# Segment 0 of a segmented-attention block: whole instead of halves, queries and keys in w2's space, scores in loose bank pairs, a new instruction order

## The chip, the core and the metric

The kernel runs on one core of one Trainium2 chip, in one launch. The metric is the device time of one execution in microseconds (us). A core has five engines with a queue each: TensorE (PE, matmuls into the eight PSUM banks; its weight loads are shown as PEld), VectorE (DVE), ScalarE (ACT), GpSimd (POOL) and SyncE (SP, which here issues DMAs). Each works through its own queue in order, and semaphores order the engines among themselves.

## The reference

One transformer block over 2048 tokens of width 640, with 32 heads of 20 columns and a feed-forward width of 1728. Attention runs in four segments of 512 tokens: causal softmax inside the segment, plus a linear memory `M`, `z` that the earlier segments have filled.

```python
x = A_x
h = x + _A_ref(_layernorm(x), wq, wk, wv, wo, beta)
h2 = h + silu(_layernorm(h) @ w1) @ w2

# inside _A_ref, for each segment s (q, k, v are the segment's)
p = softmax(q @ k.T * scale + mask)
a_dot = p @ v
num, den = phi(q) @ M, phi(q) @ z + 1e-06      # phi(t) = t + 1 if t > 0 else exp(t)
o = g * num / den + (1 - g) * a_dot            # g = sigmoid(beta)
M, z = M + phi(k).T @ v, z + sum(phi(k))
return concat(o) @ wo
```

For segment 0 the memory is empty, so only `a_dot` counts.

## The kernel before

**How the work is written down.** `build` declares tasks (a few instructions on one engine, with what they read and write) in a `Graph`. The order in which tasks are issued, the buffer each one takes and the engine of those that may run on several are written out by hand in the string `ORDER`; `Graph.schedule` reads it row by row. A row such as `qe011/D:0` is: task `qe011`, on VectorE (A ScalarE, D VectorE, G GpSimd, S SyncE), with buffer 0. `Tracker.add` then finds the semaphore waits from the regions that tasks read and write. So the order on each engine's queue is that of `ORDER`, and it never changes while the kernel runs.

**The tasks of one segment** (numbers in names: segment, then block or chunk; groups are numbered 0 to 31, eight to a segment, four heads to a group):

- `n1_st`, `n1_rs`, `n1_ap` (lines 706 to 723): layer norm of a block of 128 tokens on VectorE and GpSimd. It is transposed into `xT` by TensorE (`n1_tp`, `n1_te`, lines 732 and 741) for segment 0, by a DMA (`n1_tr`, line 747) for the others.
- `v`, `ve` (774, 784): values of a block, ten matmuls of 320 columns, and their copy into `Vx`.
- `pr`, `qe` (808, 816): one chunk of queries or keys, five matmuls of 512 columns, and its copy into `QK` on ScalarE or VectorE.
- `ex`, `ph` (823, 830, 833): phi of a chunk, an exponential on ScalarE, then a maximum (830) and a minimum of two tensors (833) on VectorE.
- `vt` (844): twelve DMA copies per segment on SyncE's queue that gather the last 12 heads' rows from `QK` into `QKV`. Groups 5 to 7 of a segment read `QKV`, groups 0 to 4 `QK`.
- `qk`, `e`, `mk` (880, 891, 903): one score visit, four heads side by side on TensorE into four adjoining PSUM banks; two exponentials on ScalarE, a pair of banks each, into a probability buffer; the causal mask on GpSimd.
- `av`, `oe`, `tn`, `nm`, `ad` (926, 939/941, 955 and 959, 972 to 1000): probabilities times values, copy out, turn to tokens (with the memory part, from segment 1 on), division, sum into `otok`.
- `kt`, `mz`, `ma`, `mb` (1040 to 1084): a DMA transpose of phi(k), and the memory's update.
- `ot`, `wo`, `rs`, `n2_*` (1101 to 1117): transpose of `otok`, output projection, residual, second layer norm into `hT`.
- `h1`, `th`, `s`, `h2`, `o`, `out` (1138/1143, 1152, 1158, 1178, 1195, 1200): the feed-forward layer and the store. `h1_0_7_1` is segment 0, chunk 7, second half.

**Segment 0 is split in halves.** Its first 256 queries see only two key blocks. They have visits of their own (`0x` to `7x`, 384 columns a head, buffers `PTE`), and the other 256 queries two visits a group (`ya`, 512 columns, `PTA`; `yb`, 384 columns, `PTB`). So there are 24 visits, 16 products `av` and 16 copies `oe`, and the first layer of segment 0's feed-forward part also comes in halves of 256 tokens (`parts` in `declare_back`). From segment 1 on a group has visit `a` (512 columns), `b` (384 and 128), and every second group a visit `e` (256 for this group and 256 for the next).

**Buffers.** `PTA`, `PTB` and `PTE` have two slots each. `QK` and `xT` have one copy; a chunk of segment 1 is written into `QK` only when segment 0's visits and copies have read it. A visit asks for four adjoining banks:

```python
sca = G.alloc("ps", nr)          # nr = 4
```

**The start.** SyncE issues x blocks 0 and 1, wv, x blocks 2 and 3, beta, wq and wk, one after the other. wq and wk come raw into `sT`'s space and are rearranged (`re_`, lines 677 and 679) on ScalarE or VectorE. `fill` tasks (line 599) are matmuls of 256 columns on a tile of zeros (`zpad`), whose results nobody reads: 41 in all, 21 of them ahead of the first transpose.

Of the kernel before, what the change touches and what calls it, by code (L numbers as in the profile page):

```python
# [358 lines left out]
zpad:0 x0:0 x1:1 w_wv:0 x2:2 x3:3 beta w_q:0 w_k halfc warm:0 iota vpad0 sel n1_st0:0 n1_st1:1 epsc mt3 vpad1 n1_rs0  # L359
n1_rs1 epsg0 n1_ap0:0 fill21:0 n1_tp0:0 n1_te0/A:0 n1_ap1:1 fill6:2 n1_tp1:2 n1_te1/A v00:0 v01:2 n1_st2:2 n1_rs2  # L360
n1_st3:3 n1_rs3 mt1 mt2 mta1 n1_ap2:2 n1_ap3:3 n1_tp2:4 n1_te2/D re_wq1/A:0 fill4:6 n1_tp3:6 n1_te3/A pr010:6
re_wk1/D:0 re_wk0/D re_wk3/D x4/S:4,5,6,7 pr011:4 re_wk2/D re_wq4/D qe011/D:0 ve00/A:0 re_wk4/A qe010/A re_wq2/A
lsc0 pr001:0 ve01/D lsc1 lsc2 re_wq0/A qe001/A:0 qk1x0:4 e1x2:0 pr000:1 qe000/D lsc3 pr021:0 e1x0 mk1x qk0x0:4
pr020:2 ex001:0 qe021/A:0 e0x2:1 e0x0 qe020/A n1_st5:4 n1_st6:5 pr041:0 re_wq3/D av1x:3 qk2x0:4 w_wo/S:0
x8/A:8,9,10,11 vt06:0 vt00 vt03 vt09 qe041/D:0 pr031:1 pr030:0 n1_st4:6 n1_st7:7 w_w1_0/A:0 mk0x e2x2:0 oe1x/D:0
e2x0 ex041:1 qe030/D:0 qk0yb0:4 pr040:2 w_w1_1/S qe031/A qe040/D mk2x e0yb2:0 e0yb0 n1_rs5 av2x:0 av0x:3 tn1x:1
nm1x:0,0 oe0x/A:1 mk0yb n1_rs6 mtb1 qk1yb0:4 vt010 oe2x/D:0 vt08 vt05 vt02 vt07 vt04 e1yb2:1 e1yb0 ex021:2 zf0 v03:2
qk3x0:4 v02:0 e3x0:0 e3x2 n1_ap6:0 n1_ap5:1 ve03/D n1_tr5:0 vt011 vt01 qk4x0:4 ve02/D tn0x:2 e4x2:1 nm0x:1 e4x0 mm5
n1_rs4 fill6:3 qk0ya0:0 mta3 mk3x e0ya0:0 n1_rs7 ph001:0 mk4x e0ya2 n1_tr6 av3x:4 oe3x/D:1 n1_st8:0 ph021:1 n1_ap4:2
n1_st11:1 fill4:5 qk1ya0:4 e1ya0:1 zf1 e1ya2 v11:0 ve11/A:1 av4x:2 qk5x0:4 tn2x:3 e5x2:0 e5x0 nm2x:2 v12:0 n1_tr4  # L370
n1_ap7:3 epsg1 oe4x/D:0 ve12/D kt02:0 n1_tr7 w_w1_2/S w_w2_0/S kt00:1 w_w1_3/S ex011:0 mk1yb mk5x mt0 qk6x0:4 av0y:2
e6x0:1 e6x2 tn4x:3 oe0y/D:0 av5x:0 tn3x:1 oe5x/A:1 qk7x0:4 e7x2:0 e7x0 nm4x:3 v10:2 nm3x:0 qk2ya0:4 ph041:2
n1_st10:2 ve10/D e2ya0:0 e2ya2 n1_rs11 mta2 mk7x n1_st9:3 n1_rs10 v13:0 mk6x tn0y:2 av7x:3 ve13/D nm0y:1 qk2yb0:4
oe7x/A:0 e2yb2:0 e2yb0 tn5x:3 tn7x:0 nm7x:2 av1y:1 av6x:2 qk3ya0:4 oe6x/D:1 nm5x:3 w_w1_4/S tn6x:2 nm6x:0 ot1:0
w_w2_5/S ot0 w_w2_4/S w_w2_1/S oe1y/A:0 e3ya0:1 e3ya2 ph011:1 pr101:1 mtb3 mz02:2 mk2yb av2y:3 qk3yb0:4 e3yb0:1
e3yb2 ma02/D:0 mz00:2 tn1y:0 oe2y/D:1 n1_ap11:1 qe101/D:0 pr100:3 qk4ya0:4 e4ya0:0 e4ya2 mk3yb ex031:2 nm1y:1
qe100/D wo1:0 av3y:3 qk4yb0:4 e4yb2:0 e4yb0 ma00/D:1 tn2y:2 ex101:1 rs1 wo0:0 oe3y/D:0 n2_st1:5 nm2y:2 kt04:0 tn3y:3
n2_rs1 nm3y:3 rs0 qk5ya0:4 pr140:2 n1_rs8 mk4yb pr121:3 e5ya0:1 e5ya2 qe140/A:0 qk5yb0:4 e5yb2:1 e5yb0 ex140:0
pr141:0 av4y:2 n2_ap1:0 n2_st0:4 n2_rs0 n2_ap0:2 kt01:1 n2_tr1:0 qk6ya0:4 qe141/D mk5yb pr120:1 ph031:0 oe4y/D:1
pr111:0 qe121/D:0 e6ya0:0 e6ya2 qk6yb0:4 qe120/D ex121:2 av5y:3 n2_tr0 h1_0_7_0:1 h1_0_0_0:2 e6yb2:0 e6yb0 qk7ya0:4  # L380
# [24 lines left out]
e16e0 ad15 mk16b th0_5_1:0 mk16a qk17b0:0 vt211:0 ot6:0 s0_5_1 ph211:1 wo6:4 th0_11_1:1 s0_11_1 rs6 n2_st6:1 e17b2:1
# [48 lines left out]
def build(nc, es, A_x, A_wq, A_wk, A_wv, A_wo, A_beta, B_x, B_w1, B_w2, out):  # L454
# [303 lines left out]
    def declare_front(s):  # L758
# [4 lines left out]
        for i in range(4):  # L763
            layer_norm("n1_", 4 * s + i, X[4 * s + i], [0], xTa, xT, i, k0 + P["ln1"] + P["ln1s"] * i if s else -30 + i)
# [491 lines left out]
```

## Time and profile before

| what | value |
|---|---|
| runs of the kernel (device time) | 306.14, 306.86, 307.66 us |
| median | 306.86 us |
| span of the profiled execution, first to last instruction | 305.4 us |
| mean granted TensorE clock in that span | 0.994 |
| instructions: PE, DVE, ACT, POOL | 2876, 490, 322, 280 |
| score exponentials on ScalarE | 168: 136 of 1024 elements, 32 of 768 |
| their mean | 1027 and about 807 ns |
| TensorE's granted clock from 10 to 20 us | 0.83 |
| DMA: bytes and mean rate | 24.65 MB, 81 GB/s |

The profiled execution's span is the time between its first and its last instruction; the device time also holds what lies around them. The page gives busy time by engine, and the same in 40 slices of the span; the chain of waits follows the last instruction back through what released each step; rows by line give the number of instructions, their mean duration and what ended the engine's idle time before them. Matmuls overlap, so the duration of one is longer than the distance from its start to the next one's start.

### The profile page before, as it was taken

How to read it: one execution, taken by the hardware profiler on the slowest of the kernel's cores; microseconds unless marked ns; L12 is line 12 of the kernel's file. 1: busy time of each engine (PE TensorE's matmuls, PEld its weight loads, DVE VectorE, ACT ScalarE, POOL GpSimd, SP SyncE). 2: the span in 40 equal slices, each digit the busy share in tenths (PEclk: the TensorE clock that was granted, in tenths of full speed). 3: DMA queues.
4: the chain of work that ended last, by engine and by line, in shares of the span. 5: the costliest groups of instructions: out<-in, count | busy, mean ns of one | idle time of the engine just before them, and what ended most of it. 6: DMA issues, size and time to landing. Idle time of an engine off the chain costs nothing.

```text
span 305.4 us, 7240 instructions
## 1 busy us (share of the span) xinstructions
PE 291.0 (95%) x2876; PEld 166.5 (55%) x2900; DVE 218.7 (72%) x490; ACT 227.0 (74%) x322; POOL 143.5 (47%) x280
## 2 busy tenths in 40 slices
PE   8699898999999999999999999999999999999996
PEld 6434454555655445656654444556564466764574
DVE  5567999796788895877989878449776476934523
ACT  4488998999998979989889899978878951004410
POOL 4227754433687856536747419334973730300000
PEclk9899999999999999999999999999999999999999
DMA  6658468642264040055552400034250004242001
GB/s 197 211 195 239 75 166 223 127 97 42 90 105 80 17 62 2 1 91 76 114 146 63 67 17 19 2 64 69 39 108 2 0 2 88 64 88 86 0 24 64
DMA packets 48578, 24.65 MB, mean 81 GB/s; under 512 B 38881, under 2 KB 47457, under 8 KB 48545
## 3 DMA queue, kind: packets, MB, share of 16 engines
q1 hardware_dynamic: 47872, 23.09, 33.1%
q10 hardware_dynamic: 672, 1.10, 1.1%
q8 instruction: 23, 0.38, 0.5%
q14 instruction: 11, 0.08, 0.1%
HBM read 10.41 MB, written 2.62 MB: 43 GB/s over the span
## 4 chain that ended last, share of the span: by engine, by line
PE 72%; ACT 12%; DVE 7%; DMA 4%; issue 2%; POOL 1%; SPq 1%; DVEq 0%; ACTq 0%
PE ps_all L1178 18%; PE ps_all L1143 16%; PE ps_all L808 12%; PE ps_all L1109 7%; PE ps_all L880 6%; PE ps_all L926 5%; ACT PTA L891 4%; ACT PTB L891 3%; DMA sT<-in_A_wq_dram 3%; PE ps_all L774 2%; PE ps_all L955 2%; ACT PTE L891 2%; DMA oT<-otok 1%; PE ps_all L959 1%; PE ps_all L1048 1%
## 5 line engine op out<-in xcount | busy, mean ns | idle before, releaser
L891 ACT ACTIVATE PTA<-ps_all 128x1024 bf16<-128x1024 f32 x64 | 62.1, 1027 | 7.1 <-PE ps_all L880 6.5
L1178 PE MATMUL ps_all<-w_sb,sT 128*128 128x320 bf16 x448 | 65.2, 299 | 0.0
L891 ACT ACTIVATE PTB<-ps_all 128x1024 bf16<-128x1024 f32 (+1 forms) x64 | 58.9, 970 | 5.9 <-PE ps_all L880 5.6
L1143 PE MATMUL ps_all<-hT,w_sb 128*128 128x512 bf16 (+1 forms) x315 | 60.1, 335 | 0.9 <-issue 0.5
L1152 ACT ACTIVATE th<-ps_all 128x512 f32<-128x512 f32 (+2 forms) x70 | 34.0, 507 | 34.5 <-PE ps_all L1143 26.8
L1158 DVE SCALAR_TENSOR_TENSOR sT<-th,ps_all 128x512 bf16<-128x512 f32 (+2 forms) x70 | 38.0, 561 | 26.1 <-ACT th L1152 25.0
L903 POOL TENSOR_SCALAR_AFFINE_SELECT PTB<-PTB 128x512 bf16<-128x512 bf16 x64 | 41.2, 644 | 32.7 <-ACT PTB L891 30.4
L1178 PEld LDWEIGHTS ps_all<-w_sb,sT 128*128 128x128 bf16 x448 | 42.3, 98 | 19.3 <-issue 2.1
L1143 PEld LDWEIGHTS ps_all<-hT,w_sb 128*128 128x128 bf16 x325 | 30.3, 98 | 23.9 <-issue 1.3
L891 ACT ACTIVATE PTE<-ps_all 128x1024 bf16<-128x1024 f32 (+1 forms) x40 | 35.4, 943 | 2.2 <-PE ps_all L880 2.1
L903 POOL TENSOR_SCALAR_AFFINE_SELECT PTE<-PTE 128x512 bf16<-128x512 bf16 x40 | 25.9, 647 | 21.0 <-ACT PTE L891 19.5
L706 DVE BATCH_NORM_STATS2 stt<-x_tok 128x6 f32<-128x320 bf16 x64 | 27.9, 477 | 1.5 <-DMA x_tok<-in_A_x_dram 1.3
L808 PE MATMUL ps_all<-xT,wqr 128*128 128x512 bf16 x92 | 24.3, 391 | 3.2 <-ACT xT L741 2.4
L1109 PE MATMUL ps_all<-wo_sb,oT 128*128 128x320 bf16 x160 | 24.1, 299 | 1.0 <-DMA oT<-otok 0.7
L774 PE MATMUL ps_all<-wv_sb,xT 128*128 128x320 bf16 x160 | 24.3, 300 | 0.7 <-DMA xT<-xn_rot 0.5
L808 PE MATMUL ps_all<-xT,wkr 128*128 128x512 bf16 x94 | 24.0, 386 | 0.5 <-issue 0.3
L1000 POOL TENSOR_TENSOR otok<-on 128x320 bf16<-128x320 bf16 x24 | 19.0, 792 | 11.3 <-DVE on L992 11.3
L903 POOL TENSOR_SCALAR_AFFINE_SELECT PTA<-PTA 128x512 bf16<-128x512 bf16 x24 | 15.5, 645 | 16.6 <-ACT PTA L891 16.4
L1195 DVE SCALAR_TENSOR_TENSOR x_tok<-ps_all,x_tok 128x640 bf16<-128x640 f32 (+1 forms) x17 | 13.2, 780 | 14.1 <-PE ps_all L1178 14.0
L880 PE MATMUL ps_all<-QK 20*128 20x256 bf16 (+3 forms) x360 | 20.5, 286 | 1.7 <-ACT PTB L891 0.7
L992 DVE TENSOR_TENSOR on<-ps_all,rd 128x640 bf16<-128x640 f32 x24 | 19.8, 825 | 0.8
L817 DVE CAST QK<-ps_all 128x512 bf16<-128x512 f32 x24 | 16.3, 687 | 5.5 <-PE ps_all L808 5.1
(79 smaller groups left out, 403.5 us busy)
## 6 DMA issues: line engine op xcount, KB each, us to landing
out_dram<-x_tok SPq DMA_DIRECT2D x15, 160.0 KB, 1.9
w_sb<-in_B_w_dram SPq DMA_DIRECT2D x4, 432.0 KB, 5.8
w_sb<-in_B_w_dram SPq DMA_DIRECT2D x3, 480.0 KB, 4.3
x_tok<-in_A_x_dram SPq DMA_DIRECT2D x2, 640.0 KB, 4.7
QKV<-QK SPq DMA_DIRECT2D x16, 72.0 KB
wv_sb<-in_A_wv_dram SPq DMA_DIRECT2D x1, 800.0 KB, 4.9
sT<-in_A_wq_dram SPq DMA_DIRECT2D x1, 800.0 KB, 8.2
sT<-in_A_wk_dram SPq DMA_DIRECT2D x1, 800.0 KB, 9.9
```

What stands on the lines that cost most here:

```text
L706: T.add(DV, lambda e, hh=hh: e.bn_stats(out=stt[:, s, 6 * hh:6 * hh + 6], in_=xb[:, 320 * hh:320 * hh + 320]), reads=R((xa, xsub)), writes ...
L774: fns.append(lambda e, c=c, hh=hh: e.matmul(bank(ps, hh)[:, 0:320], lhsT=xT[:, c, 128 * i:128 * i + 128], rhs=wv_sb[:, c, 320 * hh:320 * h ...
L808: fns = [lambda e, kc=kc: e.matmul(bank(ps)[:, lo:hi], lhsT=wt[:, kc, c, :], rhs=xT[:, kc, lo:hi], start=(kc == 0), stop=(kc == NC - 1)) f ...
L880: fns.append(lambda e, j=j, o=o, r=r, q0=q0, q1=q1, qa=qa, ka=ka: e.matmul(ps_all[:, o:o + q1 - q0], lhsT=ka[32 * r:32 * r + DH, 128 * j:1 ...
L891: T.add(AC, lambda e: e.activation(out=pt[:, pta.slot, q0:q0 + 2, 0:width], in_=sc3[:, b0:b0 + 2, 0:width], func=ACT.Exp, scale=SCALE), re ...
L903: fns.append(lambda e, v=v: e.affine_select(out=v, in_=v, pattern=[[0, 4], [1, 128]], compare_op=ALU.is_ge, fill=0.0, base=0, channel_mult ...
L992: T.add(DV, lambda e: e.tensor_tensor(out=on[:, ona.slot, :, :].rearrange("p b (x e) -> p b x e", e=DH), in0=v[:, :, :, 0:DH], in1=r2.unsq ...
L1109: fns.append(lambda e, c=c, hh=hh: e.matmul(bank(ps, hh)[:, 0:320], lhsT=oT[:, c, 128 * i:128 * i + 128], rhs=wo_sb[:, c, 320 * hh:320 * h ...
L1143: fns = [lambda e, c=c: e.matmul(bank(ps)[:, lo:hi], lhsT=w1_sb[:, c, 128 * f:128 * f + 128], rhs=hT[:, c, lo:hi], start=(c == 0), stop=(c ...
L1152: T.add(AC, lambda e: e.activation(out=th[:, tha.slot, lo:hi], in_=bank(ps)[:, lo:hi], func=ACT.Tanh, scale=0.5), reads=R((ps, [0])), writ ...
L1158: T.add(DV, lambda e: e.scalar_tensor_tensor(out=sT[:, f, lo:hi], in0=th[:, tha.slot, lo:hi], scalar=1.0, in1=bank(ps)[:, lo:hi], op0=ALU. ...
L1178: fns.append(lambda e, f=f, t0=t0, fr=fr, hh=hh: e.matmul(bank(ps, hh)[:, 0:320], lhsT=sT[:, f, t0:t0 + 128], rhs=w2_sb[:, fr, 320 * hh:32 ...
```

## The change

**Segment 0 whole.** The halves are gone: segment 0 has the visits `a`, `b` and `e` of the other segments, 20 instead of 24, eight products and eight copies, and its feed-forward layer has 512 tokens to a matmul.

**Where its operands lie.** The transposed input of segment 0 goes into `hT` instead of `xT`, and its queries and keys into the first eight chunks of `w2_sb`, so that segment 1's can be written while segment 0's are read. The loads of w2 (`load_w2`) are declared behind segment 0's groups, and the first three of them wait for all readers of these queries and keys.

**Scores.** A visit takes two pairs of adjoining banks, wherever they lie, and each exponential reads one pair. The three kinds of probability buffer become one pool of seven.

**Other engines.** The maximum of phi is a task of its own (`pa`), on VectorE or GpSimd; the minimum is `pb`. The rearrangements of wq and wk may run on GpSimd, and four do.

**A new `ORDER`.** All rows are new. The four x blocks are loaded first, then wv, wk, wq, then x blocks 4 to 7, then beta. Of 49 fills 40 stand ahead of the first transpose, and the zero tile is written after the identity matrix. The feed-forward part of segment 0 begins behind the first visit of segment 1's sixth group; before, it began during segment 0's visits.

```diff
-zpad:0 x0:0 x1:1 w_wv:0 x2:2 x3:3 beta w_q:0 w_k halfc warm:0 iota vpad0 sel n1_st0:0 n1_st1:1 epsc mt3 vpad1 n1_rs0
-n1_rs1 epsg0 n1_ap0:0 fill21:0 n1_tp0:0 n1_te0/A:0 n1_ap1:1 fill6:2 n1_tp1:2 n1_te1/A v00:0 v01:2 n1_st2:2 n1_rs2
...
+mt2:0 iota sel zpad x2:2 n1_st2:7 mt0 x0:0 n1_st0:0 warm:0 mta0 epsc halfc n1_rs2 n1_ap2:3 x1:1 x3:3 fill40:0 n1_tp2:3
+n1_st1:1 n1_rs0 n1_ap0:2 w_wv:0 n1_te2/A:0 fill9:0 n1_tp0:4 w_k:0 n1_st3:2 n1_te0/A v02:0 vpad0 ve02/A:0 n1_rs1
+n1_ap1:0 n1_rs3 n1_ap3:3 n1_tp1:6 w_q v00:2 n1_te1/A mt1 re_wk0/D:0 n1_tp3:6 vpad1 v01:0 x4/S:4,5,6,7 n1_te3/D pr001:4
+re_wq0/D:0 pr000:5 re_wq4/D mt3 mta3 re_wk3/G re_wq2/D re_wk2/D beta re_wq3/G ve00/A v03:2 re_wq1/A qe001/A:0 re_wk4/G
+mta1 ve01/A n1_st4:0 ve03/D qe000/A qk0a0:0,4 n1_st5:4 ex001:1 re_wk1/G pr011:7 qe011/D:0 e0a2:5 qk0b0:2,4 mtb1 mtb0
...
+        "QZ0": 1, "QZ1": 1, "QZ2": 1, "QZ3": 1, "QZ4": 1,
-        "PTA": 2, "PTB": 2, "PTE": 2, "oTs": 2, "on": 2, "rd": 4, "otok": 1, "oT": 1,
+        "PT": 7, "oTs": 2, "on": 2, "rd": 4, "otok": 1, "oT": 1,
...
+    QK0 = w2_sb[:, 0:8, :].rearrange("p f e -> p (f e)").rearrange("p (c w t) -> p c w t", c=5, w=2)
...
-            G.task(f"re_{k}{c}", {DV: 0.36 if c < 3 else 0.42, AC: 0.72}, emit, rr, ww, prio + c)
+            G.task(f"re_{k}{c}", {DV: 0.36 if c < 3 else 0.42, AC: 0.72, PO: 0.8 if c < 3 else 0.9}, emit, rr, ww, prio + c)
...
-        xTa = G.alloc("xT")
+        xTa = G.alloc("xT" if s else "hT")
+        xt = xT if s else hT
+        qkt = QK if s else QK0
...
-        qk = [G.alloc(f"QK{c}") for c in range(5)]
+        qk = [G.alloc(f"QK{c}" if s else f"QZ{c}") for c in range(5)]
...
-                    G.task(f"ph{s}{c}{w}", {DV: 0.92}, e_phi, [(qk[c], wall), (exa, [0])], [(pa, ["a"])], prp)
+                    G.task(f"pa{s}{c}{w}", {DV: 0.37, PO: 0.65}, e_pa, [(qk[c], wall)], [(pa, ["a"])], prp)
+                    G.task(f"pb{s}{c}{w}", {DV: 0.38}, e_pb, [(exa, [0]), (pa, ["a"])], [(pa, ["a"])], prp)
...
-                sca = G.alloc("ps", nr)
+                sca = [G.alloc("ps", 2) for _ in range(nr // 2)]
+                scw = [(a, [0]) for a in sca]
...
-                            o = 512 * (sca.slot + r - r0) + co
+                            o = 512 * (sca[(r - r0) // 2].slot + (r - r0) % 2) + co
...
-        if s == 0:
-            for g in range(NG):
-                k = P["x0"] + P["xs"] * g
-                pe = scores(f"{g}x", "PTE", PTE, [(g, 0, 0, 256, 0), (g, 1, 128, 256, 256)], k, 384,
-                            [(0, 0), (1, 0)])
-                tick(g, k, f"{g}x", 0, 2, [(0, pe, PTE, 0, 0), (1, pe, PTE, 256, 128)])
-            for g in range(NG):
-                k = P["y0"] + P["ys"] * g
-                pa = scores(f"{g}ya", "PTA", PTA, [(g, 0, 256, 512, 0), (g, 1, 256, 512, 256)], k)
-                pb = scores(f"{g}yb", "PTB", PTB, [(g, 2, 256, 512, 0), (g, 3, 384, 512, 256)], k + P["qkp"], 384)
...
+        pe = None
+        for g in range(NG):
+            k = k0 + g
+            pa = scores(f"{k}a", "PT", PT, [(g, 0, 0, L, 0)], k)
+            pb = scores(f"{k}b", "PT", PT, [(g, 1, 128, L, 0), (g, 3, 384, L, 384)], k + P["qkp"])
+            if g % 2 == 0:
+                pe = scores(f"{k}e", "PT", PT, [(g, 2, 256, L, 0), (g + 1, 2, 256, L, 256)], k + 2 * P["qkp"])
...
-        parts = [(0, 2), (2, 4)] if s == 0 else [(0, 4)]
+        parts = [(0, 4)]
...
+    def load_w2():
+        for k, (f0, f1) in enumerate(((0, 4), (4, 7), (7, 10), (10, 13))):
+            old = [(a, WH) for a in segs[0]["qk"]] if k < 3 else []
+            load_w(f"w2_{k}", w2_sb[:, f0:f1, :], cw(B_w2[128 * f0:128 * f1, :]), 2 + k, 0.45 * (f1 - f0),
+                   [(W["w2"], [k])] + old)
+
...
+        if s == 0:
+            load_w2()
```

More of the change, by code (lines that the diff above doesn't have):

```diff
@@ L364 @@
[L364 to L368, printed above, removed]
@@ L822, in e_ex @@
                     def e_ex(eng, c=c, w=w, exa=exa, wall=wall):
-                        T.add(AC, lambda e: e.activation(out=ex[:, exa.slot, :], in_=QK[:, c, w, :], func=ACT.Exp),
+                        T.add(AC, lambda e: e.activation(out=ex[:, exa.slot, :], in_=qkt[:, c, w, :], func=ACT.Exp),
                               reads=R((qk[c], wall)), writes=R((exa, [0])))
@@ L1098, in declare_back @@
             b = 4 * s + i
-            pr = (P["wox"] if s == 0 and i < 2 else k0 + P["wo"]) + P["wos"] * i
+            pr = (k0 + P["wo"]) + P["wos"] * i
             dma(f"ot{b}", [(ot, [(i, g) for g in range(NG)])], [(oTa, [i])],
@@ L1132, in declare_back @@
                 tha = G.alloc("th")
-                pr = (P["h1x"] if q == 0 and s == 0 else k0 + P["h1"]) + P["h1s"] * f
+                pr = (k0 + P["h1"]) + P["h1s"] * f
                 def e_mm(eng, f=f, tail=tail, ps=ps, lo=lo, hi=hi, b0=b0, b1=b1):
```

225 lines of the change are left out of this document (106 added, 119 removed).

## The prediction

> **What bounds the kernel now.** First the page's busy shares, then six stretches cut at score visits (the start up to the first one, then one stretch for each segment's visits, then the rest), then the chain that ended last.
>
> ```profile
> PE 291.0 (95%) x2876; PEld 166.5 (55%) x2900; DVE 218.7 (72%) x490; ACT 227.0 (74%) x322; POOL 143.5 (47%) x280
> ...
> PE 72%; ACT 12%; DVE 7%; DMA 4%; issue 2%; POOL 1%; SPq 1%; DVEq 0%; ACTq 0%
> ```
>
> ```profile
> core 0: us, PE busy (x) PEld busy (x) DVE busy (x) ACT busy (x) POOL busy (x), PEclk, DMA share, GB/s
> 0.00:18.30 18.30, 14.68 (x86) 8.96 (x88) 10.40 (x33) 9.05 (x17) 6.10 (x25) 0.91 0.63 206
> 18.30:71.00 52.70, 49.28 (x605) 26.13 (x609) 43.70 (x118) 49.08 (x72) 27.23 (x55) 1.00 0.60 153
> 71.00:123.80 52.80, 51.28 (x569) 29.03 (x574) 41.53 (x94) 48.88 (x67) 36.00 (x76) 1.00 0.30 55
> 123.80:186.70 62.90, 60.85 (x601) 34.02 (x606) 52.66 (x111) 57.32 (x83) 33.87 (x59) 1.00 0.36 70
> 186.70:242.30 55.60, 54.81 (x591) 30.56 (x595) 37.03 (x76) 47.46 (x62) 32.89 (x55) 1.00 0.22 42
> 242.30:305.40 63.10, 60.14 (x442) 37.77 (x445) 33.34 (x60) 15.18 (x26) 7.45 (x14) 1.00 0.19 50
> ```
>
> TensorE is busy in over 93% of every stretch after the start, and ScalarE is close behind it in segment 0's (49.08 of 52.70). Since matmuls overlap, I weigh TensorE by the spacing of its matmuls instead of by busy time:
>
> ```profile
> 20.84 0.34 PE L880 MATMUL ps_all<-QK 20*128 20x256 bf16 x8
> 21.11 1.25 PE L808 MATMUL ps_all<-xT,wqr 128*128 128x512 bf16 x5
> ```
>
> ```profile
> 75.17 1.09 PE ps_all L1143 x10
> ...
> 290.43 12.35 PE ps_all L1178 x90
> ```
>
> A 256-column matmul takes 109 ns (1.09 over 10), a 320-column one 137 (12.35 over 90), so a column takes 0.42 ns and 512 columns 216 ns. The score visit at 20.84 streams 256 and then 128 columns, four matmuls side by side: 0.16 us. The next run starts 0.27 after it: a switch from one kind of run to another costs about 0.11.
>
> TensorE's own work in the kernel before, from the program's instruction list: L1178 448 x 0.136 = 60.9; L774 and L1109 320 x 0.136 = 43.5; L808 200 x 0.216 = 43.2; L1143 195 x 0.216 + 130 x 0.109 = 56.3; its tails (L1138) 2.1; scores and probability products 32 groups x 1280 columns each = 34.1; L955 and L959 10.3; L1048 5.2; transposes 1.1; fills 41 x 0.109 = 4.5. Sum 261.2. There are 330 runs, at 0.096 on average 31.7 of switches. Together 292.9 of the span's 305.4: 12.5 us are lost, 7.5 in the start (18.3 less 10.8 of work, fills included) and only 5.0 in the 287 us after it. So TensorE bounds the kernel; a cheaper ScalarE does not by itself shorten it.
>
> **The change, part by part.**
>
> *Halves to whole.* Segment 0 keeps its columns. 130 matmuls of 256 columns become 65 of 512 (14.2 to 14.0), ScalarE's 32 exponentials of 768 and 16 of 1024 elements become 40 of 1024. The list has 307 runs instead of 330: the 23 that go are mostly score visits (84 to 80), probability products (36 to 31) and unloads (39 to 31), at 0.11 each 2.5 us. Fills go from 41 to 49 (+0.9, in the start). TensorE's work: 261.1 + 0.9 + 31.7 - 2.5 = 291.2.
>
> *ScalarE* loses 8 of 16 key/query copies (0.6 each, 4.8), 5 half and 4 whole output copies (5.2), 25 half tanh for 13 whole ones (2.4), three of four weight rearrangements (2.9) and two DMA issues (1.0). That is 16 us of work, but it lies beside TensorE and I give it nothing except where ScalarE would bind. It does in one place. From the first score visit to that of segment 1's sixth group (the front) the new list has 65 exponentials. This row
>
> ```profile
> 34.08 3.78 ACT L891 ACTIVATE PTA<-ps_all 128x1024 bf16<-128x1024 f32 x4
> ```
>
> shows four in 3.78, 0.91 apart when back to back: 59; with 15 exponentials of keys and queries at 0.52 and two copies ScalarE has 67.7. TensorE's own work there is 65.9, as segment 0's feed-forward now begins only after the front. Before, the same groups (18.3 to 100.0) held 77.6 of TensorE work in 81.7, 95%. With two engines that close I take 70.5 (TensorE 93%, ScalarE 96%): 4.6 lost. Bounds: 67.7 (ScalarE never waits) and 77 (six more us of waits). After the front TensorE has 210 left; before it lost 0.9 after the same point, and I keep that.
>
> *Bank pairs and seven buffers.* A visit waits for two free pairs instead of four adjoining banks. The waits of ScalarE for score matmuls are 6.5 + 5.6 + 2.1 = 14.2 us in the whole run, those of TensorE's weight loads for exponentials 14.7. But of 84 visits 65 were followed by the next run after just the switch. Over that, visits lost 5.3 us, already within the 12.5. Bounds 0 to -5.3; I take nothing, as the front gets denser.
>
> *The start.* Rows on how it goes now:
>
> ```profile
> 1.12 4.66 PE L599 MATMUL ps_all<-zpad 128*128 128x256 bf16 x21 [1.12 <-DVE zpad L578]
> ...
> 10.94 0.45 PE L732 MATMUL ps_all<-ident,xn_rot 128*128 128x128 bf16 x5
> 13.77 1.91 PE L808 MATMUL ps_all<-xT,wqr 128*128 128x512 bf16 x4 [2.38 <-ACT xT L741]
> 15.48 2.89 PE L808 MATMUL ps_all<-xT,wkr 128*128 128x512 bf16 x10
> ```
>
> 21 fills at 222 ns (slow clock), then faster; an idle gap before 13.77; then matmuls of 512 columns 427 ns apart (15.48 less 13.77, over four), twice 216: the slow clock again. After: all four x tiles are issued first (issues 0.47 apart, each x 0.4 to 0.5 to land after 3.09: the last by 4.5), then wv (3.0: by 7.5), wk and wq (2.2 each: by 12). beta's tiny rows, between 7.42 and 9.60 now, go behind them. The zero tile waits behind the index tile and the 0.78 us identity on VectorE, so the fills start at about 2.15 instead of 1.12. Forty of them, 23 slow (5.1, as long as now) and 17 at 0.109: until 9.1. Then nine more fills 1.0, four transposes 1.3, four value projections 5.6 and two key/query projections 2.2, all back to back since the weights have landed: first visit at 19.2. The list's start holds 14.5 of work, so 4.7 are lost instead of 7.5. Bounds: forty fast fills 16.7, forty slow ones 21.2.
> In the Trainium skill, TensorE: Matmul & The Clock Gate, Part 1, the clock rises after one busy window of 3.4 us whose edges are independent of the kernel: between 3.4 and 6.8 us after the first fill. By that the sum would be 0.8 lower or higher; the first fast fill here, about 5 us after the first one, lies in that interval.
>
> *GpSimd* gets 13 of 30 maxima (L830) (no row; between the select's 0.63 and the two-input add's 0.79 for 320 elements, so 1.2 for 512; I take 0.65, nearest in kind) and four rearrangements (rows of copies: 84 elements 0.28; about 1.0 each). In the front it then has 57 of 70.5 and VectorE, by the spacing of its rows, 60. The rearrangements end by about 15, and the projection that first needs one comes after the first score visit. So they cost nothing; without that cover a late maximum holds the transpose and the state product behind it, and what stands behind that product on TensorE.
>
> *SyncE's queue.* Three loads of w2 now wait for the last reader of segment 0's queries and keys, the fifth group's shared visit. Behind the first of them stand wo and segment 1's state transposes, needed two to four groups (10 to 20 us) later; w2 itself is needed ten groups later: hidden. The 12 copies into QKV must land before that same visit, which is the nearer date (rival 2).
>
> **The sum.** 291.2 + 4.7 + 4.6 + 0.9 = 301.4 of span, against 305.4. The median of the runs, 306.86, is 1.5 over the span (the three runs 0.7 to 2.3); I keep that: 302.9. A change below 0.5% (1.5 us) this measurement can't tell from none: same is 305.3 to 308.4.
>
> **Rivals.**
> 1. *Clean front.* Pairs and buffers take the 5.3 of waits out and ScalarE runs through: front 67.7, and the clock rises early (first visit 17.5). 291.2 + 3.0 + 1.8 + 0.9 = 296.9, time 298.4. For it: the 14.2 us ScalarE now waits for scores. Against: after any visit the wait moves to whichever engine frees the pair. 0.20.
> 2. *Late QKV (slower).* The list has 10.6 of TensorE work from the first visit to the last projection of segment 0 and 24.1 to the shared visit; at 95% these are 30.4 and 44.6. From 30.4 SyncE has 11 copies at 0.68, three transposes at 1.25 and 2 us to land: 43.6. Its queue is in order, so a late copy stops everything behind it, one for one. From 1.0 us of delay on it costs. A copy took up to 1.60 to issue beside weight loads (24 us into the span); 11 at 1.3 are 6.8 late, 5.8 of it on the path: front 76.3, time 308.7, and 310 with one more late transpose. Against: the weight loads now stand behind these copies. 0.17.
> 3. *VectorE and GpSimd hold each other.* The front has both at over 80%. The two-input minimum (L833) took 424 ns at best, 894 at worst, 470 more; 14 such and 9 GpSimd maxima at 0.47 are 10.8, VectorE 71 of 70.5: front 75, time 307. 0.12. In the Trainium skill, SBUF — State Buffer, section SBUF: two separate sides, the two engines share a pair of ports that one instruction holds for its whole length, so moving work to GpSimd can stop VectorE; the stretched rows agree with it.
>
> ```profile
> L833 DVE TENSOR_TENSOR phiK<-phiK,ex x15: 424/425/798, 33.8 to 182.0; 128x512 bf16<-128x512 bf16 x15
> L833 DVE TENSOR_TENSOR phiQ<-phiQ,ex x15: 424/426/894, 83.0 to 224.5; 128x512 bf16<-128x512 bf16 x15
> ```
>
> That the change doesn't do what it says can't be: the lists show it.
>
> **Chances.** Forecast (299.5 to 305.3) 0.51, clean front 0.20, ports 0.12, late QKV 0.17. Faster is the first two: 0.71; same 0.12; slower 0.17. The range takes in rival 1 with its lower bound for the start (16.7, 0.8 less: 297.6, and 1 for the waits after the front) and most of rival 2: 296.5 to 309.5.
>
> **What would show it.** Right: first score visit at 18.4 to 20; no matmul at half clock after the fills; the front 68 to 73 with ScalarE over 90% busy in it; under 2 us lost after it; a span near 301. Wrong: the front over 74, with the fifth group's shared visit waiting for the queue (rival 2) or VectorE over 95% there (3); or TensorE waits after the front, which no term allows for.

## The result and the profile after

The changed kernel takes 315.9 us (median of 314.64, 315.44, 316.36, 317.26) against 306.5 for the kernel before, run beside it: ratio 1.0313, 95% interval [1.0271, 1.0356]. The forecast was 302.9. The profiled execution is the one of 314.64 us; its span is 312.6, against 305.4 before. Its granted TensorE clock was 1.00 throughout, and two of the other three runs had 0.989.

The page of the changed kernel, busy time by engine and the chain that ended last by engine:

```profile
PE 288.2 (92%) x2675; PEld 158.5 (51%) x2705; DVE 221.9 (71%) x452; ACT 216.6 (69%) x276; POOL 172.9 (55%) x304
...
PE 60%; DVE 13%; POOL 11%; ACT 7%; DMA 5%; issue 3%; SPq 1%; ACTq 0%; POOLq 0%
```

TensorE's share of the chain fell from 72 to 60%, GpSimd's rose from 1 to 11 and VectorE's from 7 to 13, and GpSimd is busy 29 us longer. Where the time went is seen when both executions are cut at the same places: the first score visit, and the first visit of segment 1's sixth group. First the kernel before:

```profile
core 0: us, PE busy (x) PEld busy (x) DVE busy (x) ACT busy (x) POOL busy (x), PEclk, DMA share, GB/s
0.00:18.30 18.30, 14.68 (x86) 8.96 (x88) 10.40 (x33) 9.05 (x17) 6.10 (x25) 0.91 0.63 206
18.30:100.00 81.70, 77.64 (x920) 42.91 (x926) 66.71 (x173) 76.89 (x112) 47.65 (x104) 1.00 0.54 127
100.00:305.40 205.40, 198.73 (x1873) 114.59 (x1890) 141.56 (x287) 141.02 (x194) 89.78 (x152) 1.00 0.25 51
```

Then the changed kernel:

```profile
0.00:18.02 18.02, 16.27 (x119) 11.66 (x122) 11.82 (x33) 8.99 (x13) 10.91 (x41) 1.00 0.75 237
18.02:97.19 79.17, 66.88 (x716) 32.46 (x726) 67.56 (x146) 70.77 (x84) 68.29 (x118) 1.00 0.60 127
97.19:312.63 215.44, 205.04 (x1844) 114.41 (x1863) 142.47 (x273) 136.81 (x180) 93.68 (x147) 1.00 0.23 48
```

The start is 0.3 us shorter, the front 2.5 shorter and the rest 10.0 longer: 7.2 together, the difference of the spans. Now compare TensorE's busy time inside the front: 77.64 of 81.70 before, 66.88 of 79.17 after. Some 11 us of TensorE's work left the front, but the front hardly became shorter. These rows by line, of the kernel before from 18.3 to 100 us, show the largest part of what left:

```profile
L1178 PE MATMUL ps_all<-w_sb,sT 128*128 128x320 bf16 x56 | 8.7, 300 | 0.0
L1143 PE MATMUL ps_all<-hT,w_sb 128*128 128x256 bf16 x65 | 8.4, 273 | 0.0
```

It is the feed-forward layer of segment 0's first 256 tokens: 56 x 0.137 and 65 x 0.109 are 14.8 us of columns. With a whole segment it can't start until all eight groups are through, and it runs after the front. In exchange some 4 us of projections came into the front (21 chunks of queries and keys there, 17 before). Behind the front TensorE was busy for 198.73 of 205.40 us before and for 205.04 of 215.44 now: 6.3 of the 10.0 us that this part grew are work, 3.7 are idle time. That the moved work makes the first share is read from these sums; no run left it out there.

The other news is on GpSimd, the maximum's line in the changed kernel (duration in ns: least, median, most):

```profile
L825 POOL TENSOR_SCALAR phiK<-QK x5: 1912/1921/1927, 38.0 to 137.4; 128x512 bf16<-128x512 bf16 x5
L825 POOL TENSOR_SCALAR phiQ<-QK x5: 1919/1925/2105, 68.1 to 202.1; 128x512 bf16<-128x512 bf16 x5
L825 POOL TENSOR_SCALAR phiK<-w_sb x3: 1927/2001/2049, 19.0 to 30.8; 128x512 bf16<-128x512 bf16 x3
```

A maximum takes 1.9 to 2.1 us there, not 0.65; nine of the thirteen are in the front.

### The profile page after: what moved, and what is told of

Its sections match the earlier page's. It is cut to its first block, busy times and chain, and to the rows that moved or that the text cites. A ratio compares the mean times of both kernels' runs of the same rounds, so it can differ in the third digit from the quotient of the medians.

```text
span 312.6 us, 6838 instructions
## 1 busy us (share of the span) xinstructions
PE 288.2 (92%) x2675; PEld 158.5 (51%) x2705; DVE 221.9 (71%) x452; ACT 216.6 (69%) x276; POOL 172.9 (55%) x304
## 4 chain that ended last, share of the span: by engine, by line
PE 60%; DVE 13%; POOL 11%; ACT 7%; DMA 5%; issue 3%; SPq 1%; ACTq 0%; POOLq 0%
PE ps_all L1168 18%; PE ps_all L1133 16%; ACT PT L894 5%; PE ps_all L1099 5%; PE ps_all L881 4%; PE ps_all L803 4%; POOL PT L906 4%; POOL phiK L825 4%; PE ps_all L929 3%; PE ps_all L769 3%; PE ps_all L594 2%; PE ps_all L958 2%; DMA phiKt<-phiK 2%; DVE stt L699 2%; DMA oT<-otok 2%
## 5 line engine op out<-in xcount | busy, mean ns | idle before, releaser
L894 ACT ACTIVATE PT<-ps_all 128x1024 bf16<-128x1024 f32 x160 | 154.7, 1024 | 25.9 <-PE ps_all L881 24.8
L906 POOL TENSOR_SCALAR_AFFINE_SELECT PT<-PT 128x512 bf16<-128x512 bf16 x128 | 82.7, 654 | 55.9 <-ACT PT L894 52.2
L1133 PE MATMUL ps_all<-hT,w_sb 128*128 128x512 bf16 x247 | 58.7, 380 | 1.8 <-DVE sT L1148 0.8
L1142 ACT ACTIVATE th<-ps_all 128x512 f32<-128x512 f32 (+1 forms) x56 | 31.3, 584 | 39.4 <-PE ps_all L1133 32.7
L1148 DVE SCALAR_TENSOR_TENSOR sT<-th,ps_all 128x512 bf16<-128x512 f32 (+1 forms) x56 | 35.9, 664 | 23.9 <-ACT th L1142 23.7
L929 PE MATMUL ps_all<-PT,Vx 128*32 128x384 bf16 (+3 forms) x512 | 23.1, 302 | 2.7 <-POOL PT L906 1.6
L944 DVE TENSOR_SCALAR oTs<-ps_all,lsc 128x512 bf16<-128x512 f32 x26 | 19.3, 742 | 6.1 <-PE ps_all L929 5.9
L1099 PEld LDWEIGHTS ps_all<-wo_sb,oT 128*128 128x128 bf16 x160 | 15.0, 97 | 9.7 <-issue 2.2
L710 POOL TENSOR_TENSOR rst<-rst,eps_c 128x1 f32<-128x1 f32 x32 | 18.3, 572 | 2.5
L716 DVE TENSOR_SCALAR xn_rot<-x_tok,mvt,rst 128x640 bf16<-128x640 bf16 x32 | 16.9, 532 | 2.5 <-POOL rst L710 2.3
```

Of the source, the lines that this page charges most:

```text
L894: T.add(AC, lambda e: e.activation(out=pt[:, pta.slot, q0:q0 + 2, 0:width], in_=sc3[:, b0:b0 + 2, 0:width], func=ACT.Exp, scale=SCALE), re ...
L906: fns.append(lambda e, v=v: e.affine_select(out=v, in_=v, pattern=[[0, 4], [1, 128]], compare_op=ALU.is_ge, fill=0.0, base=0, channel_mult ...
L929: fns.append(lambda e, j=j, r=r, h=h, pa=pa, pt=pt, co=co, q0=q0, ji=ji: e.matmul(bank(po)[32 * r:32 * r + 32, q0:hi], lhsT=Vx[:, vx.slot, ...
L1099: fns.append(lambda e, c=c, hh=hh: e.matmul(bank(ps, hh)[:, 0:320], lhsT=oT[:, c, 128 * i:128 * i + 128], rhs=wo_sb[:, c, 320 * hh:320 * h ...
L1133: fns = [lambda e, c=c: e.matmul(bank(ps)[:, lo:hi], lhsT=w1_sb[:, c, 128 * f:128 * f + 128], rhs=hT[:, c, lo:hi], start=(c == 0), stop=(c ...
L1142: T.add(AC, lambda e: e.activation(out=th[:, tha.slot, lo:hi], in_=bank(ps)[:, lo:hi], func=ACT.Tanh, scale=0.5), reads=R((ps, [0])), writ ...
```

## The experiments

"Front" is the stretch from the first score visit to that of segment 1's sixth group, with TensorE's granted clock in it. Ratios are against the kernel before, run on the same chip.

| kernel | front, us (clock) | ratio to the kernel before, 95% interval |
|---|---|---|
| the changed kernel | 79.2 (1.00) | 1.0313 [1.0271, 1.0356] |
| max_vector | 82.2 (0.98) | 1.0278 [1.0223, 1.0334] |
| rearr_vector | 84.9 (0.94) | 1.0391 [1.0349, 1.0432] |
| max_short | 77.3 (0.98) | 1.0180 [1.0131, 1.0230] |
| max_one_stage | 80.1 (0.96) | 1.0233 [1.0197, 1.0268] |
| loads_behind | 78.9 (1.00) | 1.0221 [1.0194, 1.0249] |
| phik4 | 78.1 (1.00) | 1.0296 [1.0252, 1.0340] |
| max_vector_phik4 | 77.7 (1.00) | 1.0253 [1.0228, 1.0278] |
| all3 | 79.0 (0.98) | 1.0257 [1.0200, 1.0314] |
| e_light | 84.2 (0.94) | 1.0381 [1.0348, 1.0413] |
| dve_light | 79.3 (1.00) | 1.0323 [1.0284, 1.0362] |
| pool_light | 78.3 (0.98) | 1.0414 [1.0360, 1.0469] |
| all_light | 81.4 (0.96) | 1.0374 [1.0299, 1.0450] |
| loads_late | 79.4 (1.00) | 1.0516 [1.0471, 1.0561] |
| loads_late_mv4 | 76.4 (1.00) | 1.0480 [1.0419, 1.0541] |
| loads_late_light | 72.4 (1.00) | 1.0371 [1.0320, 1.0422] |
| loads_early_mv4 | 76.8 (0.98) | 1.0183 [1.0129, 1.0238] |
| before_less_ff | 82.7 (0.96), 81.7 before | 1.0011 [0.9980, 1.0041] |
| after_more_fill | 83.8 (1.00) | 1.0410 [1.0346, 1.0473] |

A front is read from one execution. Where the clock is below 1.00, TensorE ran part of it at half clock; that accounts for at most (1 - clock) x front, so some 1.6 us at 0.98 and 5 at 0.94. Behind the front the order is the same in all kernels made from the changed one, but the length there was 213.3 to 217.0 us (the late kernels aside): differences of 2 us between single executions show nothing.

**The price of the maxima.** Four kernels from the changed one.

```diff
# max_vector: all 13 in ORDER
-pa001/G:2 ... pa340/G:0
+pa001/D:2 ... pa340/D:0
# rearr_vector
-re_wk3/G re_wq3/G re_wk4/G re_wk1/G
+re_wk3/D re_wq3/D re_wk4/D re_wk1/D
# max_short
-e.tensor_scalar(out=o, in0=qkt[:, c, w, :], scalar1=0.0, scalar2=1.0, op0=ALU.max, op1=ALU.add)
+nn = 160 if eng == PO else L
+e.tensor_scalar(out=o[:, 0:nn], in0=qkt[:, c, w, 0:nn], scalar1=0.0, scalar2=1.0, op0=ALU.max, op1=ALU.add)
-e.tensor_tensor(out=o, in0=o, in1=ex[:, exa.slot, :], op=ALU.min)
+e.tensor_tensor(out=o, in0=qkt[:, c, w, :], in1=ex[:, exa.slot, :], op=ALU.min)
# max_one_stage, on GpSimd
-scalar1=0.0, scalar2=1.0, op0=ALU.max, op1=ALU.add
+scalar1=0.0, scalar2=None, op0=ALU.max
```

> The 13 maxima of phi go from GpSimd to VectorE, at the same places in the order. Theory A (the price: a maximum took 1.95 us on GpSimd and not 0.65; late maxima hold VectorE, the masks and the state): a maximum takes 0.28 to 0.9 us on VectorE, the front falls from 79.2 us to 70 to 74, the time from 315.9 to 305 to 309. Theory B (VectorE and GpSimd stretch each other, the price of one does not matter): the two-input minimum falls from 0.55 to under 0.45 us on average and the front falls by as much as these stretches sum to, under 5 us: time 311 to 314. Theory C (four rearrangements on GpSimd delay what follows): 315, no change. Theory D (the order itself leaves TensorE waiting): over 312.

> The four rearrangements of wq and wk on GpSimd go to VectorE, the maxima stay. Theory A: 315 to 318, nothing gained, since VectorE is then later by 1.5 to 2.5 us in the start. Theory C: they delay the first maxima and the masks behind them on GpSimd's queue; 312 to 314.

> The maxima stay on GpSimd, but do 160 of 512 columns (the minimum reads the chunk itself, so that what the maximum leaves out is not read): the price that the forecast assumed, with the same waits. Expected 0.6 to 0.7 us for one maximum. Theory A: the front comes to the 70.5 to 74 us of the forecast, time 305 to 309, as in the kernel with the maxima on VectorE. Theory B: the stretches of VectorE's rows stay in part; 311 to 314. Theory D: over 312.

> The maxima stay on GpSimd with all 512 columns, but leave out the addition of 1 (one operation in place of two). If the price comes from the second operation, one takes about 1.0 us and by theory A the time falls by half of what the other kernels gain, to 309 to 312. If it comes from the elements or their type, 1.9 us and 315 to 316.

The maximum's line, first in max_short, then in max_one_stage:

```profile
L825 POOL TENSOR_SCALAR phiK<-QK x5: 738/744/750, 36.2 to 135.3; 128x160 bf16<-128x160 bf16 x5
```

```profile
L825 POOL TENSOR_SCALAR phiK<-QK x5: 1477/1483/1492, 37.3 to 138.9; 128x512 bf16<-128x512 bf16 x5
```

With 0.74 us, close to the price of the forecast, the kernel is 1.3% faster than the changed one (1.0180 against 1.0313, some 4 us) but still 1.8% slower than before, and its front is 77.3, not 70.5. So theory A names a real cost and not the main one. With one operation in place of two a maximum takes 1.48 us: the second operation is 0.44 us of the price, and most of the rest goes by elements (160 of them with both operations take 0.74). Moving the maxima to VectorE can't be told from no gain: the intervals of the ratios overlap. Its chain of waits, from 52 to 66 us, shows one wait that the move brought (start, length, what):

```profile
52.72 0.46 DVE phiK L831
53.21 6.49 DMA phiKt<-phiK
59.72 0.62 DVE phiK L825
60.35 0.66 DVE oTs L944
```

The maximum at 59.72 waits for a buffer of phi(k), which comes free only when a state transpose lands, 6.49 us after its issue. On GpSimd only GpSimd waited there; on VectorE the unloads and copies behind it wait too. One wait was exchanged for another; whether that ate the whole gain is tried next. Moving the rearrangements to VectorE gains nothing: the second visit comes at 23.1 instead of 19.5. The half clock there can make up the rest of the difference, so the runs show no cost of theirs on GpSimd. Theory C falls.

**The late transposes.** Five loads moved on SyncE's queue, a fourth buffer, or both.

```diff
# loads_behind, all3
-... w_w1_0/S ... w_w2_0/S ... w_w1_2/S ... w_w2_5/S ... w_wo/S:0 ... kt10:0 ... kt11:1
+... kt10:0 ... kt11:1 w_wo/S:0 w_w1_0/S w_w2_0/S w_w1_2/S w_w2_5/S
# phik4, max_vector_phik4, all3: slots of pa..1 in ORDER dealt anew
-"pK": 3
+"pK": 4
# max_vector_phik4, all3: the maxima on /D
```

> Five weight loads (wo, two parts of w1, two of w2) go on SyncE's queue from ahead of the first two state transposes of segment 1 to behind them; the maxima stay on GpSimd. Theory E (burst): six loads issued from 44.2 to 48.2 us are still moving at 55, the transposes behind them need 7.2 and 5.1 us to land, and the buffer of phi(k) that the second one frees holds the next maximum (start 56.9), with all behind it on GpSimd and VectorE. Then the two transposes land in 2.3 to 3, that maximum starts 2 to 3 us earlier, the front is 76 to 77.5 in place of 79.2, and the time 312.5 to 314.5. Rival D (the order leaves TensorE waiting elsewhere): 315.5 and more, the same.

> Four buffers of phi(k) in place of three; the maxima stay on GpSimd, no instruction moves. Theory E: no maximum waits for a transpose any more, the same gain as with the loads behind (front 76 to 77.5, 312.5 to 314.5). If the slow transposes count through the state product on TensorE and not through the buffer, 315 to 316.

> The maxima on VectorE, and four buffers of phi(k). Theory F (with three buffers, moving the maxima only exchanged one wait for another: VectorE itself then waits for the late transpose, with the evictions of queries and keys queued behind it, 57.4 to 61.8 us at the seventh group's visit): without the buffer wait the gain of the cheaper maximum shows, front 82.2 to 75 to 78, time 315.4 to 308 to 311. Rival D: 314 and more.

> The maxima on VectorE, four buffers of phi(k) and the five loads behind the transposes. Theories E and F together: front 73 to 76, time 305.5 to 309. Rival D: over 312.

What they act on, in the changed kernel: its chain from 49 to 66 us, and the DMAs issued from 43 to 53 (number, KB each, us to landing).

```profile
51.78 5.09 DMA phiKt<-phiK
56.95 1.92 POOL phiK L825
59.05 1.89 POOL phiK L825
60.95 0.42 DVE phiK L831
```

```profile
wo_sb<-in_A_wo_dram SPq DMA_DIRECT2D x1, 800.0 KB, 7.1
...
phiKt<-phiK SPq DMA_TRANSPOSE x3, 5.1
```

With the loads behind, the two transposes land in 2.3 and 2.4 us, the kernel gains 0.9% (some 2.8 us), and the time is what theory E asked for. But its mechanism isn't there: the maximum that theory E had 2 to 3 us earlier starts at 56.67 in place of 56.95, now behind two masks and a layer norm step on GpSimd, and the front is 78.9. So the time came out by luck, and the place of the gain isn't shown. The fourth buffer alone can't be told from nothing, nor, by the intervals, from what it gives with the maxima on VectorE (1.0253); theory F holds at most in part. All three together are no better than two: 79.0. With the wait for the buffer gone, or the two slow transposes, or both, the front is still 78 to 79.

**Is it any engine's work?** Work is left out of each engine in the front, at the same order.

```diff
# e_light: groups 3 to 12
-out=pt[:, pta.slot, q0:q0 + 2, 0:width], in_=sc3[:, b0:b0 + 2, 0:width]
+out=pt[:, pta.slot, q0:q0 + 2, 0:wd], in_=sc3[:, b0:b0 + 2, 0:wd]    # wd = width // 2
# dve_light: n1 of blocks 4 to 11, n2 of blocks 0 to 3
-in_=xb[:, 320 * hh:320 * hh + 320]
+in_=xb[:, 320 * hh:320 * hh + 32]
# pool_light: groups 0 to 12
-v = pt[:, pta.slot, :, co:co + 128]     # pattern [[0, 4], [1, 128]]
+v = pt[:, pta.slot, 0:1, co:co + 128]   # pattern [[0, 1], [1, 128]]
# all_light: all three
```

> In the front (groups 3 to 12) each score exponential does 256 of 512 columns a head, the rest is left out; the order, the waits and all other work stay. ScalarE loses some 50 x 0.43 = 21 us of the 70.8 it is busy in the front. Theory G1 (ScalarE bounds the front, as the forecast had it, with 67.7 of work): the front falls from 79.2 to 70 or less, time 307 or less. Theory G2 (GpSimd bounds it: 57 by the forecast and 1.3 more for each of nine maxima, 68.7): 77 to 79, time 314 to 316. Theory G4 (no engine alone, each waits for another in turn): 1 to 4 us.

> In the front the statistics of the layer norms read 32 of 320 elements (24 instructions, 0.42 us less each: VectorE loses some 10 us of the 67.6 it is busy there); the rest stays. If VectorE bounds the front: 79.2 to 70 to 73. G2: no change. G4: 1 to 4 us.

> In the front (groups 0 to 12) the causal masks do one head of four (some 50 instructions, 0.45 us less each: GpSimd loses some 22 us of the 68.3 it is busy there); the maxima stay. G2: the front falls to 71 to 74, time 308 to 311. G1: 78 to 79. G4: 1 to 4 us.

> All three at once: exponentials halved, short statistics, masks of one head. TensorE's work in the front stays 65.9. G4: the front falls by far more than any one alone, to 66 to 70, time 303 to 307. Theory G5 (the front is held by the length of the handoffs from engine to engine and by transposes in flight, not by the engines' work): still over 74.

None gains anything: the fronts are 78 to 84, and 76.6 to 79.3 if all that the half clock can cost is taken off. (pool_light's four runs lay far apart, 314.2 to 319.6. The profiled one is the shortest, and the two shortest are on average 1.031 times the kernel before, so the 1.0414 of the table doesn't show that it lost time.) The stretch of all_light, and below it the same kernel with the weight loads moved away (next paragraph):

```profile
17.90:99.30 81.40, 70.36 (x728) 33.24 (x727) 58.33 (x149) 50.70 (x84) 51.30 (x118) 0.96 0.59 123
```

```profile
18.80:91.20 72.40, 67.21 (x724) 32.34 (x723) 58.44 (x146) 50.59 (x84) 50.28 (x116) 1.00 0.43 82
```

ScalarE went from 70.8 to 50.7 us, GpSimd from 68.3 to 51.3 and VectorE from 67.6 to 58.3, and the front didn't follow. (In dve_light alone VectorE lost 5.2 us, to 62.3, and not the 10 expected.) Theories G1 and G2 fall, and G4 with them in the form it had: work of three engines together wasn't enough either.

**Is it the transfers?**

```diff
# loads_late, loads_late_mv4, loads_late_light: from their places in ORDER to behind n2_tr1
+w_w1_1/S w_w1_3/S w_w1_0/S w_w1_2/S w_w1_4/S w_w2_4/S w_w2_5/S w_w2_0/S w_w2_3/S w_w2_1/S w_w2_2/S
# loads_early_mv4: w1 and w2_4, w2_5 behind x8, the rest of w2 behind n2_tr1
# ..._mv4: maxima on /D, "pK": 4.  loads_late_light: the edits of all_light
```

> The loads of w1 and w2 go on SyncE's queue behind the last transpose of the front; wo stays where it was; the maxima stay on GpSimd. The feed-forward part must then wait for w1 (2.2 MB, some 9 us at the 237 GB/s of the start), so the time is 315 to 325 by itself; what counts is the front. Theory G5a (transposes slowed by weight loads hold the front): all transposes land in 2.3 to 2.9 us and the front falls from 79.2 to 72 to 75. G5b (the bare length of the handoffs): 77 to 79.

> The same with the maxima on VectorE and four buffers of phi(k). G5a: front 69 to 73, the value of the forecast. G5b: 76 to 78, as with the maxima on VectorE and four buffers alone (77.7).

> Loads late, exponentials halved, short statistics, masks of one head. If transfers and engines hold the front together it falls to TensorE's own 66 to 69. If it stays over 74, the bare length of the chain of handoffs holds it.

> w1 and the two small parts of w2 are loaded right behind x blocks 8 to 11, at some 20 us; the four large parts of w2 behind the front; maxima on VectorE, four buffers of phi(k). G5a: the stretch from 18 to 35 us is 2 to 4 us longer, the rest of the front shorter by more: front 73 to 77, time 306 to 311. G5b: 312 to 315.

Alone, no: 79.4 without a single load of w1 or w2 in the front, though 19 of its 26 transposes there land in 2.3 to 2.7 us (the others in 3.2 to 4.7). (The times of the three late kernels hold the wait for w1 behind it.) With cheaper maxima 76.4, with the three engines' work cut 72.4, where the expectation had 66 to 69 if transfers and engines held it together and over 74 if the handoffs did. It lies between: the two cover each other, for the cut in the engines' work gained nothing alone and some 7 us here, but even with both gone the front is 6.5 us over TensorE's 65.9. loads_early_mv4 is, with loads_behind (1.0221), the best complete version found (1.0183), and slower than the kernel before.

**Was the feed-forward work free?** The last two runs turn the question round.

```diff
# before_less_ff, in the kernel before: segment 0's first half
-for c in range(NC)]                    # first layer, five matmuls a tile
+for c in range(nc1)]                   # nc1 = 1
-for f in range(f0, f1):                # second layer, fourteen tiles a block
+for f in ([f0] if b < 2 and q < 3 else [NF - 1] if b < 2 else range(f0, f1)):
# after_more_fill, in ORDER of the changed kernel: ahead of 3a, 4b, 5a, 6a, 6e, 7b, 8a, 9a, 10a, 10e, 11b, 12b
+fill8:0 qk3a0:2,0
```

> The kernel before, with most of the feed-forward matmuls of segment 0's first 256 tokens left out: one of five in the first layer (13 tiles x 4 x 0.109 = 5.7 us), four of fourteen in the second (2 blocks x 10 x 2 x 0.136 = 5.4): 11.1 us less of TensorE, all tasks, waits and other engines' work stay. Theory H (handoffs hold this stretch, the feed-forward work was filler in TensorE's gaps): from the first visit to segment 1's sixth group 81.7 us become 78 or more, time 302.5 to 306. Rival I (TensorE bounds the kernel before, as the forecast read it): the stretch falls by 9 to 11 us, time 295 to 298.

> The changed kernel with twelve runs of eight 256-column matmuls on the tile of zeros put ahead of twelve visits of the front, in banks that are free there (12 x 0.87 = 10.5 us of TensorE). Theory H: the gaps take most of it, front 79.2 to 80 to 84, time 316 to 320. Rival I: the front grows by 9 to 11 us, time 325 to 327.

before_less_ff, in the three stretches:

```profile
0.00:16.60 16.60, 13.11 (x87) 7.99 (x89) 10.31 (x33) 8.82 (x17) 6.10 (x25) 1.00 0.64 194
16.60:99.29 82.69, 70.61 (x828) 34.52 (x834) 67.12 (x173) 76.80 (x113) 47.75 (x104) 0.96 0.56 132
99.29:304.28 204.99, 198.61 (x1873) 114.64 (x1890) 141.47 (x287) 140.97 (x194) 89.75 (x152) 1.00 0.24 51
```

11.1 us of TensorE's work left out of the kernel before don't change its time measurably: 1.0011 [0.9980, 1.0041]. The stretch is 82.7, of which the half clock can be 3.3: 79.4 to 82.7, where rival I asked for 71 to 73. Its chain from 60 to 99 us has ScalarE's exponentials in front (second line), where the whole kernel, from 60 to 100, has TensorE (first line):

```profile
by line: PE ps_all L1178 20.3%; PE ps_all L1143 9.6%; ACT PTA L891 9.2%; PE ps_all L808 8.1%; PE ps_all L880 7.7%; PE ps_all L1109 7.5%; ACT PTB L891 7.0%; PE ps_all L926 4.5%; ACT th L1152 3.6%; DVE QK L817 3.0%; DVE oTs L941 2.6%; DVE x_t
by line: ACT PTA L891 20.4%; ACT PTB L891 18.2%; PE ps_all L1109 10.9%; issue 10.1%; PE ps_all L880 7.1%; ACT th L1152 5.5%; PE ps_all L926 4.8%; ACT ex L823 4.2%; ACT PTE L891 3.4%; PE ps_all L1178 3.3%; DVE QK L817 3.1%; DVE oTs L941 2.7%
```

These are its engines from 60 to 87 us:

```profile
60.00:75.00 15.00, 11.66 (x156) 5.58 (x151) 11.78 (x30) 14.62 (x25) 5.71 (x11) 1.00 0.31 75
75.00:87.00 12.00, 7.03 (x83) 3.16 (x82) 9.66 (x26) 11.89 (x18) 9.28 (x28) 0.98 0.36 84
```

ScalarE is busy for 26.5 of the 27 us, TensorE for 18.7. In the kernel before both were busy for 26.4 of the same 27. So theory H is right that the feed-forward work was filler there; that handoffs hold this stretch isn't shown. ScalarE may set it, and no run of the kernel before left out ScalarE's work.

And with 10.5 us of idle matmuls put into the changed kernel's front, it grows by 4.7, at full clock:

```profile
17.77:101.60 83.83, 76.80 (x811) 41.62 (x819) 67.76 (x149) 70.86 (x84) 68.43 (x120) 1.00 0.60 125
```

In this execution more than half went into gaps. So between the visits TensorE has time to give away, in both kernels, and the kernel before used it for 14.8 us of feed-forward work. No run put useful work into the front of the changed kernel.

## Why the prediction was wrong, point by point

The span came out at 312.6 where the sum had 301.4: 8.7 us more in the front, 3.7 more behind it, 1.2 less in the start.

*What bounds the kernel now.* This is the step that failed. The forecast took a stretch in which TensorE is busy for 95% as one that TensorE sets ("TensorE bounds the kernel"), and took the work that left that stretch off its length. Part of that work only filled gaps: 11.1 us of it taken away changed the time by nothing measurable and the stretch by at most 2.3 us. For that stretch of the kernel before the forecast gave TensorE's 77.6 of 81.7 us alone; ScalarE was busy for 76.9 of the same 81.7.

*The front.* "With two engines that close I take 70.5", with bounds of 67.7 and 77: it was 79.2, 8.7 over the value and 2.2 over the bound. The sum let the front shrink with TensorE's work (65.9) and ScalarE's (67.7), as if the larger of two sums set it. The runs at full clock showed 76 to 80 with the work of one engine cut, or transfers moved, or the maxima made cheaper. By busy time ScalarE had 70.8 there, 3.1 over its sum; that is 89% of the front and not 96%, and cutting it gained nothing (e_light).

*After the front.* Forecast 301.4 - 19.2 - 70.5 = 211.7, measured 215.4. The 3.7 too little are TensorE's waits, which the forecast names as a sign of being wrong: it is idle for 10.4 us there, 6.7 before. The longest are for the transpose of `otok` (1.6, before 0.7), for masks on GpSimd (1.6, before 0.6) and for a transpose of x (1.1, before none). What makes them stays open: the kernels with the same order there had 213.3 to 217.0, with cheap late maxima (213.4 in max_short, 216.1 in max_vector_phik4) and with dear ones (213.5 in loads_behind).

*The start* was 1.2 us better than forecast: first visit at 18.0 in place of 19.2, no half clock after the fills.

*Halves to whole* was right in its counts, and wrong to price them alone: the edit also made segment 0's feed-forward wait for the whole segment. The forecast named that move, but gave it no cost, since it counted TensorE's work wherever it lies.

*GpSimd's maxima* were mis-sized: 0.65 taken, 1.2 as the upper bound, 1.92 measured. What they took over 0.74 us cost some 4 us (max_short). The forecast chose the price by kind, from the select; even its upper bound, by elements from the two-input add, was too low. The Trainium skill, GPSIMD Engine Reference, section 4.1, Engine selection, sends an elementwise maximum to VectorE, as the measurements would; its remark that one-input work runs at roughly line-rate on GpSimd doesn't fit 1.92 us beside the 0.28 to 0.29 us that the same maximum takes on VectorE when undisturbed.

*The rearrangements* were right as far as shown: moving them off GpSimd gained nothing (rearr_vector).

*SyncE's queue.* "Hidden" was too much said. Six loads issued within 4 us are moving together, and the transposes behind them land after up to 7.2 us. Moving five of them behind the transposes gained some 2.8 us (loads_behind), though not by the wait that was expected.

*The rivals.* Late QKV didn't happen: the fifth group's shared visit ran at 46.0 with no wait for the queue. VectorE and GpSimd do stretch each other's rows, as before the change (the two-input minimum took 409 to 933 ns), but VectorE was busy 85% of the front, and 5.2 us less of its work gained nothing (dve_light). The clean front is refuted. None of them was the mechanism: the list of rivals lacked the one that what was taken out of the stretch had been nearly free.

What stays open: how the 13 us between TensorE's 65.9 and 79.2 divide among the maxima, the transposes and the handoffs. They overlap, and their shares don't add up. The bank pairs, the seven buffers and the start's order weren't tried alone.

## What to carry to other kernels

A busy share near 100% doesn't show that an engine sets the time of a stretch: see whether another engine is as busy there, leave some of the work out and see whether the stretch shrinks, before you credit a change with that work. Independent work that an engine does between dependent steps can be nearly free where it is and cost much of its length in a place with fewer gaps, so price a move by the gaps at both ends. And where several chains are nearly as long as one another, removing any one of them may show its price only after the others are gone.

## What the runs showed of the hardware that was not expected

With less work TensorE ran slower. In before_less_ff it was busy for 1.3 us of 4 from 81 to 85 us (longest idle 1.4), and for 1.59 of the 3.42 us up to 86.6; from there it ran at half clock for 6.8 us:

```profile
81.00:83.00 2.00, 0.68 (x8) 0.38 (x9) 1.47 (x6) 1.95 (x4) 0.63 (x1) 1.00 0.33 74
83.00:85.00 2.00, 0.62 (x9) 0.23 (x11) 1.97 (x5) 2.00 (x3) 1.80 (x6) 1.00 0.52 99
...
87.00:88.00 1.00, 0.73 (x9) 0.26 (x10) 0.95 (x3) 1.00 (x3) 1.00 (x2) 0.50 0.69 135
```

In e_light the same follows an idle gap of 2.9 us; the timeline of its TensorE shows ten matmuls of 320 columns in 2.85 us, where ten take 1.5 at full clock:

```profile
88.18 2.85 PE L1099 MATMUL ps_all<-wo_sb,oT 128*128 128x320 bf16 x10 [2.90 <-DMA oT<-otok]
```

The Trainium skill, TensorE: Matmul & The Clock Gate, Part 1, has the clock fall after at least one idle window of some 3.4 us. Neither case had one: the longest idle gaps are 2.9 and 1.4 us. In the twenty traces of this case the granted clock, whose steps come a multiple of 3.41 us apart, fell 23 times from 1.00 to 0.50, each time behind 3.41 us in which TensorE was busy for 56% or less. Each of these 3.41 us stretches that was busy for less than 43% was followed by a fall; of those from 44 to 56% some were. So experiments that relieve an engine have to be read beside the clock, and idle matmuls between visits may be worth their time. That wasn't tried for its own sake: in after_more_fill they didn't pay (1.0410 against 1.0313, with overlapping intervals; the clock of its runs was 0.995 to 1.00, that of the changed kernel's 0.989 to 1.00).
